# Pacing every load of an attention-plus-FFN kernel by the landing of earlier loads

## The chip, the core and the metric

The kernel runs on one core of a Trainium2 chip. A core has a matrix engine (TensorE, PE in the profile), a vector engine (VectorE, DVE), an activation engine (ScalarE, ACT), GpSimd (POOL) and a queue engine (SyncE, SP); PE, DVE and ACT work on on-chip memory, which 16 DMA engines fill from and empty to device memory (HBM). DMA transfers are issued by an engine's instruction stream: here POOL issues nearly all loads, SP the transposes and stores, ACT a few transfers at the start and one at the end. The metric is the device time of one execution in microseconds (us). Before: 283.06 us, the median of three runs (282.26 to 284.77).

## The reference

Attention with a block mask over 4 batches, 8 heads, 768 positions and 64 channels per head, followed by a gated feed-forward layer on the 3072 rows of 512 channels:

```python
scores = (q @ k.T) / 8                                  # per batch and head, 768 x 768
mask   = |bi - bj| <= 1 or bi, bj in {0, 23} or bj in sampled_blocks[bi]   # blocks of 32
attn   = softmax(where(mask, scores, -1e9)) @ v
x      = attn as (4*768, 8*64)
out    = (sigmoid(x @ w_gate) * (x @ w_val)) @ w_out    # 512 -> 1536 -> 512
```

All inputs but the sampled block numbers are float32, and so is the output. The inputs that are loaded are q, k and v (6.3 MB each) and the three weight matrices (3.1 MB each).

## The kernel before

The matrix products run in float16. The work is cut into 12 units (4 batches by 3 stretches of 256 queries). For each unit and each of 4 pairs of heads, three steps compute scores (`qk`), exponentiate them on ACT (line 570) and multiply by the mask on DVE (line 576; in the first unit the mask is added on PE as a bias instead). Then the product with v, which carries a column of ones for the sum, is taken on PE, divided by that sum on DVE (lines 615 and 616) and transposed into `xT`: by PE in the first two units, after that by a DMA transpose on SP (line 667). The feed-forward part follows in groups of one or two units: `f` multiplies `xT` with columns of `wg` and `wv`, takes tanh on ACT (line 762) and gates on DVE (line 765) into `ht`; `y` multiplies `ht` with `wo`, and ACT or DVE (lines 831 and 833) evacuate the result, which SP stores (line 823). Nearly all matrix products go through the helper `tiled`, so the profile puts them down to line 338.

The order of the instructions on every engine is written out by hand in the string `ORDER`: `Plan.run` walks it and emits each task at its place. A token such as `215@30` means that task 215, a load, also waits for task 30, a score product, so that later batches' loads don't all start at once (`hold`). The order on each engine is thus fixed, and an engine that waits at one instruction holds back all that stand behind it.

Three helpers issue the loads, all on POOL's queue, where each changes float32 to float16 on the way:

- `load_heads` (line 220): two heads of q, k or v. The first batch's q comes in two parts, tiles 0 and 1, and tiles 2 to 5.
- `load_w` (line 230): 256 columns of `wg` and the same 256 of `wv`, two transfers.
- `load_wo` (line 235): four of the twelve row blocks of `wo`.

The loads of the first batch and of the weights are issued up front in the order of the string `FIRST`:

```python
FIRST = "k1 q1 v0 k2 q2 v1 k3 q3 v2 v3 r0 w0 r1 w1 r2 w2 r3 w3 w4 w5 o0 o1 o2"
```

k, q, v and r are k, the first part of q, v and the rest of q, with the number of the pair of heads; w and o are `load_w` and `load_wo`. The first pair's k and q (`kp` in the profile, as they pass through that buffer) come by SP and ACT in float32. Loads of the later batches are tasks of `ORDER`; each waits until its buffer is free, that is, until PE or DVE has read what the last batch left in it (`copies[nm, b - 1, p]`). In batches 1 to 3 a load of q or k is then paired up on DVE (`pair_up`, line 509) and transposed by SP (`xbar`, line 520), and a load of v is copied into `vex` (`vcopy`, line 529). In the first batch, PE transposes q and k (lines 451 and 456).

POOL does nothing in this kernel but set four constants and issue 66 transfers: a small spread matrix (`e<-bb_spread`) and 65 loads. The completion of POOL's transfers is told by eight semaphores, used in turn, so in the program as it is built nearly every transfer from the ninth on waits for the one eight places earlier, besides what its buffer makes it wait for.

Of the kernel before, what the change touches and what calls it, by code (L numbers as in the profile page):

```python
# [22 lines left out]
NT = S // 128  # L23
# [11 lines left out]
BIG = 1024.0  # L35
FIRST = "k1 q1 v0 k2 q2 v1 k3 q3 v2 v3 r0 w0 r1 w1 r2 w2 r3 w3 w4 w5 o0 o1 o2"
FFN_LAG = 3
VW = 96
ORDER = """
j3 j3 j3 j3 0 j3 j3 j3 11D 1:0 8A 3:1 5D 12:2 6:3 4A 7D 2 13A 80:3 106:1 9:0 30:2 107A 10D 81D  # L40
# [114 lines left out]
def kernel(  # L155
# [11 lines left out]
    nc = tc.nc  # L167
# [45 lines left out]
    v16 = sing.tile([128, H, NT, D], f16)  # L213
    vex = [sing.tile([128, H, NT, VW], f16, name=f"vex{r}") for r in range(2)]
    qT = [sing.tile([128, NP, S], f16, name=f"qT{r}") for r in range(2)]
    kT = [sing.tile([128, NP, S], f16, name=f"kT{r}") for r in range(2)]


    def load_heads(dst, src, b, h0, h1, t0=0, t1=NT):
        return nc.gpsimd.dma_start(  # L220
            dst[:, h0:h1, t0:t1, :],
            src[b, h0:h1].rearrange("h (p t) d -> p h t d", t=NT)[:, :, t0:t1, :],
        )

    W_AT = (0, 2, 4, 6, 8, 10, 12)

    def load_w(j):
        f0, f1 = W_AT[j] * 128, W_AT[j + 1] * 128
        for dst, src in ((wg, moe_w_gate), (wv, moe_w_val)):
            nc.gpsimd.dma_start(  # L230
                dst[:, :, f0:f1], src.rearrange("(c p) f -> p c f", p=128)[:, :, f0:f1]
            )

    def load_wo(j):
        nc.gpsimd.dma_start(
            wo[:, 4 * j : 4 * j + 4, :],
            moe_w_out.rearrange("(f p) m -> p f m", p=128)[:, 4 * j : 4 * j + 4, :],
        )

    mc = const[0:NB, 128:].bitcast(f32).rearrange("a (n c) -> a n c", c=4)  # L240
    sbi = sing.tile([NB, 3], mybir.dt.int64)
# [16 lines left out]
    for name in FIRST.split():  # L258
        j = int(name[1])
        if name[0] == "w":  # L260
            load_w(j)
        elif name[0] == "o":
            load_wo(j)
        else:
            dst, src, t0, t1 = {
                "k": (k16, k, 0, NT),
                "v": (v16, v, 0, NT),
                "q": (q16, q, 0, 2),
                "r": (q16, q, 2, NT),
            }[name[0]]  # L270
            load_heads(dst, src, 0, 2 * j, 2 * j + 2, t0, t1)
# [41 lines left out]
    def idle(unit):  # L313
        for i in range(2):
# [4 lines left out]
                start=True,  # L319
                stop=True,  # L320
            )

    def wait_for(ins, earlier, reason):
        tc.add_manual_dep(
            ins,
            earlier.name,
            mybir.DependencyInfo(mybir.DependencyClass.Sync, mybir.DependencyReason.DATA),
            reason=reason,
        )

    plan = Plan(
        ORDER,
        idle,
        lambda load, scored: wait_for(load.ins, scored, "loads spread over the batch before"),
    )

# [3 lines left out]
    def turns(mms, bank, first, begins=True, ends=True):  # L340

        if not first and begins:
            wait_for(nc.tensor.nop().ins, bank.last, "row tiles change banks")
        for n, job in enumerate(mms):
            for row in range(2):
                out, lhsT, rhs = job(row if first else 1 - row, slice(row * D, (row + 1) * D))
                bank.last = tiled(
                    out,  # L350
                    lhsT,
                    rhs,
                    first and begins and n == 0,
                    not first and ends and n == len(mms) - 1,
                )
# [590 lines left out]
    loads = deque()  # L946

    def later(b):
# [3 lines left out]
        def load(nm, p):  # L952
            src, dst = {"k": (k, k16), "q": (q, q16), "v": (v, v16)}[nm]
            ld = plan.add(
                [(DMA, 0.72)],
                lambda eng: load_heads(dst, src, b, 2 * p, 2 * p + 2),
                copies[nm, b - 1, p],
                dma=("L", 0.393),
                gated=True,
            )  # L960
            preps.append(lambda: follow(nm, p, ld))
# [74 lines left out]
    for n in range(1, len(units)):  # L1036
# [5 lines left out]
        for sl in range(6):  # L1042
# [3 lines left out]
            if loads:  # L1046
                loads.popleft()()
            part = parts.popleft() if n > 1 or sl >= FFN_LAG else []
            for i, fn in enumerate(part):
# [53 lines left out]
```

## Time and profile before

| | |
|---|---|
| median of three runs | 283.06 us (282.26 to 284.77) |
| the profiled execution's own time | 281.96 us |
| its span, first to last instruction | 280.2 us |
| PE busy | 272.4 us (97%) |
| DVE / ACT / POOL busy | 187.9 / 192.1 / 47.4 us |
| POOL's queue: packets, data, share of the 16 DMA engines' span | 21552, 13.93 MB, 35.6% |
| SP's and ACT's queue (`hardware_dynamic`, q1) | 34592, 13.99 MB, 22.7% |
| median time from issue to landing: k / q / v | 5.9 / 7.1 / 5.5 us |
| the same for wg / wv / wo | 8.6 / 8.9 / 12.8 us |

The profile is of one execution. "Span" is measured from its first to its last instruction. A row of digits shows the span in 40 slices of 7 us: each digit is the busy share of the slice in tenths. "PEclk" is the share of the full TensorE clock that was granted. The chain that ended last is followed back from the last instruction, at each step to whatever released it. In a list of waits, a row such as `A <- B: 1.1, 1, 1.1` says that A's engine sat idle before A until B released it: 1.1 us in total, once, 1.1 us at the longest. "To landing" is the time from the issue of a transfer to its completion semaphore. In the answer on one tile, `x1: 706/706/706, 31.4 to 31.4` is the number of instructions, their shortest, median and longest duration in ns, and when the first and the last of them started. Matmuls are pipelined and their ends are modelled.

### The profile page before, as it was taken

What the parts mean: (1) busy time and instruction counts of PE and PEld (TensorE: products, weight loads), DVE (VectorE), ACT (ScalarE), POOL (GpSimd) and SP (SyncE); (2) the same over time, 40 slices, a digit from 0 to 9 for tenths busy, and PEclk for the clock granted to TensorE, in tenths of its full rate; (3) what the DMA queues carried; (4) which work ended last, traced back from release to release, by engine and by line L of the source; (5) the groups of instructions that cost most, each with busy time, mean ns of one, the idle gap of its engine ahead of it and who ended that gap; (6) DMA issues with size and microseconds to landing.
All of it is one profiled execution on the core that took longest, in us unless ns stands there. A gap on an engine that the chain in (4) does not pass through costs nothing.

```text
span 280.2 us, 10875 instructions
## 1 busy us (share of the span) xinstructions
PE 272.4 (97%) x4889; PEld 186.1 (66%) x4889; DVE 187.9 (67%) x387; ACT 192.1 (69%) x239; POOL 47.4 (17%) x70
## 2 busy tenths in 40 slices
PE   5999999999999999999999999999999999999995
PEld 2677786777899799766555655666656667555543
DVE  4667894788887888688778746875664888142421
ACT  3798888699897878898668866578677683023301
POOL 8975441011531000082400000000000000000000
PEclk9799999999999999999999999999999999999999
DMA  7999999765589975279967330041100012440003
GB/s 148 184 195 196 200 205 202 110 127 87 77 110 150 206 129 126 40 106 188 125 115 162 68 97 2 12 133 50 30 2 0 6 21 65 117 180 2 0 5 147
DMA packets 56679, 28.92 MB, mean 103 GB/s; under 512 B 33044, under 2 KB 53676, under 8 KB 56632
## 3 DMA queue, kind: packets, MB, share of 16 engines
q0 software_dynamic: 21552, 13.93, 35.6%
q1 hardware_dynamic: 34592, 13.99, 22.7%
q8 instruction: 38, 0.62, 0.9%
q10 hardware_dynamic: 488, 0.30, 0.4%
q14 instruction: 9, 0.07, 0.1%
HBM read 28.47 MB, written 6.29 MB: 124 GB/s over the span
## 4 chain that ended last, share of the span: by engine, by line
PE 91%; DMA 3%; ACT 2%; DVE 2%; issue 1%; SPq 0%; DVEq 0%
PE m L338 89%; DMA xT<-x 2%; DMA e<-bb_spread 1%; ACT P L570 1%; PE m L456 1%; DVE ysb L833 1%; ACT ysb L831 0%; PE m L451 0%; DVE kT L282 0%; DVE mask L282 0%; ACT mask L280 0%; SPq L667 0%; PE m L397 0%; DVE x L616 0%; PE m L315 0%
## 5 line engine op out<-in xcount | busy, mean ns | idle before, releaser
L570 ACT ACTIVATE P<-m 128x1024 f16<-128x1024 f32 x144 | 142.5, 1025 | 31.3 <-PE m L338 27.3
L338 PE MATMUL m<-xT,wv 64*128 64x512 f16 (+2 forms) x672 | 136.1, 331 | 0.3 <-issue 0.3
L338 PE MATMUL m<-xT,wg 64*128 64x512 f16 (+2 forms) x672 | 135.9, 331 | 0.1
L576 DVE TENSOR_TENSOR P<-P,mask 128x1024 f16<-128x1024 f16 x132 | 86.7, 686 | 11.1 <-ACT P L570 10.8
L338 PEld LDWEIGHTS <-wg 64*128 64x128 f16 (+1 forms) x672 | 61.8, 94 | 20.5 <-issue 2.0
L338 PEld LDWEIGHTS <-wv 64*128 64x128 f16 (+1 forms) x672 | 61.8, 94 | 15.9 <-issue 0.3
L338 PE MATMUL m<-wo,ht 64*128 64x512 f16 (+2 forms) x564 | 70.7, 372 | 0.0
L765 DVE SCALAR_TENSOR_TENSOR ht<-th,m 128x512 f16<-128x512 f32 x72 | 49.0, 686 | 30.6 <-ACT th L762 29.6
L762 ACT ACTIVATE th<-m 128x512 f32<-128x512 f32 x72 | 42.7, 598 | 36.0 <-PE m L338 35.3
L338 PE MATMUL m<-qT,kT 64*128 64x256 f16 x576 | 54.0, 272 | 0.3 <-DVE ysb L833 0.2
L338 PEld LDWEIGHTS <-P 64*128 64x128 f16 (+1 forms) x2112 | 46.2, 94 | 9.0 <-issue 1.1
L338 PE MATMUL m<-vex,P 64*128 64x65 f16 (+1 forms) x2112 | 48.2, 190 | 0.0
L338 PEld LDWEIGHTS <-ht 64*128 64x128 f16 (+1 forms) x564 | 30.5, 94 | 21.6 <-issue 1.3
L338 PEld LDWEIGHTS <-kT 64*128 64x128 f16 x576 | 27.4, 95 | 13.0 <-issue 1.7
L220 POOL DMA_DIRECT2D v<-in_v_dram x16 | 11.4, 717 | 65.3 <-PE m L338 56.5
L616 DVE TENSOR_TENSOR x<-m,rz 128x256 f16<-128x256 f32 x48 | 20.4, 425 | 1.7
L615 DVE RECIPROCAL rz<-m 128x4 f32<-128x4 f32 x48 | 8.7, 180 | 17.9 <-PE m L338 16.4
L220 POOL DMA_DIRECT2D q<-in_q_dram x19 | 13.6, 723 | 12.1 <-PE m L338 11.1
L831 ACT ACTIVATE ysb<-m 128x512 f32<-128x512 f32 x13 | 7.5, 597 | 10.6 <-PE m L338 9.9
L833 DVE TENSOR_SCALAR ysb<-m 128x512 f32<-128x512 f32 x9 | 6.1, 688 | 11.8 <-ACT ysb L831 5.5
L220 POOL DMA_DIRECT2D k<-in_k_dram x15 | 10.8, 723 | 6.1 <-PE m L338 5.5
L338 PE MATMUL m<-bias,e 64*128 64x256 f16 x48 | 6.9, 301 | 0.3
(46 smaller groups left out, 69.7 us busy)
## 6 DMA issues: line engine op xcount, KB each, us to landing
out_dram<-ysb SPq DMA_DIRECT2D x23, 256.0 KB, 2.4
v<-in_v_dram POOLq DMA_DIRECT2D x16, 192.0 KB, 5.5
k<-in_k_dram POOLq DMA_DIRECT2D x15, 192.0 KB, 5.9
q<-in_q_dram POOLq DMA_DIRECT2D x12, 192.0 KB, 7.1
wg<-in_moe_w_gate_dram POOLq DMA_DIRECT2D x6, 256.0 KB, 8.6
wv<-in_moe_w_val_dram POOLq DMA_DIRECT2D x6, 256.0 KB, 8.9
wo<-in_moe_w_out_dram POOLq DMA_DIRECT2D x3, 512.0 KB, 12.8
xT<-x SPq DMA_TRANSPOSE x40, 3.2
```

The lines of the kernel that those rows point to most:

```text
L220: return nc.gpsimd.dma_start(dst[:, h0:h1, t0:t1, :], src[b, h0:h1].rearrange("h (p t) d -> p h t d", t=NT)[:, :, t0:t1, :],)
L338: return nc.tensor.matmul(out, lhsT, rhs, start=start, stop=stop, skip_group_check=True).ins
L456: nc.tensor.transpose(out16[a * D : (a + 1) * D, h, i * D : (i + 1) * D], tile_[rows, a], ident[rows, rows],)
L570: nc.scalar.activation(self.pt.rearrange("a h i n -> a (h i n)"), both(self.bank).rearrange("a h n -> a (h n)"), AF.Exp, bias=0.0, scale=SCALE
L576: nc.vector.tensor_tensor(self.pt, self.pt, m.unsqueeze(1).broadcast_to([128, 2, 2, UQ]), op=ALU.mult,)
L615: nc.vector.reciprocal(rz, self.acc[:, :, :, D : D + 1])
L616: nc.vector.tensor_tensor(self.x16.rearrange("a s h d -> a h s d"), self.acc[:, :, :, 0:D], rz.broadcast_to([128, 2, 2, D]), op=ALU.mult,)
L762: nc.scalar.activation(th, both(bank)[:, 0, :], AF.Tanh, bias=0.0, scale=0.5)
L765: nc.vector.scalar_tensor_tensor(self.ht[:, tiles[0] : tiles[-1] + 1, :], in0=th.rearrange("a (f n) -> a f n", n=self.w), scalar=1.0, in1= ...
L831: nc.scalar.activation(ysb, both(bank)[:, s, :], AF.Copy, bias=0.0, scale=0.5)
L833: nc.vector.tensor_scalar(ysb, in0=both(bank)[:, s, :], scalar1=0.5, scalar2=None, op0=ALU.mult)
```

## The change

Every load that goes through the three helpers is now handed to `paced`. It keeps a list, `sent`, of all loads in the order of issue, each with a nominal time in us: 1.0 for two heads (a third of it or two thirds for the parts of the first batch's q), 256/188 = 1.36 for 256 columns of a weight, 2.56 for a part of `wo`. For a new load, `paced` walks back over `sent` and adds up these times; the first load at which the sum of the later ones is at least `AHEAD` = 3.6 is the one whose landing the new load waits for. So at most about five loads of heads, four to five of weights, or three of `wo` are in flight.

The wait stands on POOL's queue, in front of the load, beside the waits for its buffer and for its semaphore. `FIRST`, `ORDER`, the buffers, the sizes of the transfers and everything on the other engines stay as they are. In the program as it is built, k3 (the seventh load) is the first that waits for another, for k1; the number of POOL's instructions is the same, and so are the order and the waits on PE, DVE, ACT and SP.

```diff
+AHEAD = 3.6
...
+    sent = []
+
+    def paced(load, us):
+
+        left = 0.0
+        for earlier, t in reversed(sent):
+            if left >= AHEAD:
+                wait_for(load.ins, earlier, "loads in flight")
+                break
+            left += t
+        sent.append((load.ins, us))
+        return load
+
     def load_heads(dst, src, b, h0, h1, t0=0, t1=NT):
-        return nc.gpsimd.dma_start(
+        load = nc.gpsimd.dma_start(
             dst[:, h0:h1, t0:t1, :],
             src[b, h0:h1].rearrange("h (p t) d -> p h t d", t=NT)[:, :, t0:t1, :],
         )
+        return paced(load, 1.0 * (t1 - t0) / NT)
...
     def load_w(j):
         f0, f1 = W_AT[j] * 128, W_AT[j + 1] * 128
         for dst, src in ((wg, moe_w_gate), (wv, moe_w_val)):
-            nc.gpsimd.dma_start(
+            load = nc.gpsimd.dma_start(
                 dst[:, :, f0:f1], src.rearrange("(c p) f -> p c f", p=128)[:, :, f0:f1]
             )
+            paced(load, (f1 - f0) / 188)
...
     def load_wo(j):
-        nc.gpsimd.dma_start(
+        load = nc.gpsimd.dma_start(
             wo[:, 4 * j : 4 * j + 4, :],
             moe_w_out.rearrange("(f p) m -> p f m", p=128)[:, 4 * j : 4 * j + 4, :],
         )
+        paced(load, 2.56)
```

`wait_for`, which adds such a wait, stood further down and is moved up unchanged.

More of the change, by code (lines that the diff above doesn't have):

```diff
@@ L216, with wait_for @@
     kT = [sing.tile([128, NP, S], f16, name=f"kT{r}") for r in range(2)]
+    def wait_for(ins, earlier, reason):
+        tc.add_manual_dep(
+            ins,
+            earlier.name,
+            mybir.DependencyInfo(mybir.DependencyClass.Sync, mybir.DependencyReason.DATA),
+            reason=reason,
+        )
+    sent = []
[8 more added lines that the diff above has]
+        return load
     def load_heads(dst, src, b, h0, h1, t0=0, t1=NT):
-        return nc.gpsimd.dma_start(
+        load = nc.gpsimd.dma_start(
             dst[:, h0:h1, t0:t1, :],
@@ L321, in idle @@
             )
[L323 to L329, printed above, removed]
     plan = Plan(
```

## The prediction

> **What bounds the kernel now.** I read the page's busy row first, then the chain that ended last, then the waits of POOL (the only queue that the change touches), and last, for each load, when POOL issued it and how long it took to land.
>
> ```profile
> span 280.2 us, 10875 instructions
> PE 272.4 (97%) x4889; PEld 186.1 (66%) x4889; DVE 187.9 (67%) x387; ACT 192.1 (69%) x239; POOL 47.4 (17%) x70
> ...
> PEclk9799999999999999999999999999999999999999
> DMA  7999999765589975279967330041100012440003
> ...
> PE 91%; DMA 3%; ACT 2%; DVE 2%; issue 1%; SPq 0%; DVEq 0%
> ```
>
> TensorE is busy for 97% of the span and holds 91% of the chain; the loads are on the chain only with the small `e<-bb_spread` transfer of the first 5.6 us, which the change leaves alone. Among PE's own waits the only DMA is that one, 0.8 us. So a load matters only if it lands after the instruction that reads it was due. The DMA row is at 9 from slice 2 to slice 7: for the weights, the limit is transfer rate, not issue.
>
> The transfers of the stretch from 8 to 45 us, asked for by themselves:
>
> ```profile
> DMA packets 12126, 7.32 MB, mean 198 GB/s; under 512 B 998, under 2 KB 12120, under 8 KB 12120
> ...
> q0 software_dynamic: 12120, 7.23, 136.6%
> ```
>
> Nothing but POOL's queue moves data there (the other rows of that answer are instruction fetches of 0.09 MB), at a steady 198 GB/s; SP issues nothing between 1.65 and 46.5 us.
>
> How deep is the queue now? POOL's waits say that a limit is already there:
>
> ```profile
> POOL wo L235 <- DMA wg<-in_moe_w_gate_dram: 1.1, 1, 1.1
> ...
> POOL q L220 <- DMA wo<-in_moe_w_out_dram: 0.8, 1, 0.8
> POOL wg L230 <- DMA v<-in_v_dram: 0.7, 1, 0.7
> ```
>
> These are loads that waited for the one eight places earlier: eight completion semaphores, used in turn. So before has up to eight loads in flight, not an unlimited number. What that depth does is seen in the time to landing of one load on a full and on an empty queue (the k load issued at 31.4 us, the v load issued at 120.1 us):
>
> ```profile
> L220 POOL DMA_DIRECT2D k<-in_k_dram x1: 706/706/706, 31.4 to 31.4; - x1
> DMA to landing us min/median/max: 13.0/13.0/13.0
> ```
>
> ```profile
> L220 POOL DMA_DIRECT2D v<-in_v_dram x1: 707/707/707, 120.1 to 120.1; - x1
> DMA to landing us min/median/max: 3.5/3.5/3.5
> ```
>
> The same bytes, 13.0 and 3.5 us: the difference is time spent behind other loads.
>
> **The change, step by step.** *The rule.* Each load walks back over the loads before it, adds their nominal times until 3.6 us is reached, and waits for the next one back. Loads of two heads (1.0 each) wait for the fifth before them, with 4.0 us of queued work still ahead; weight columns (1.36 each, mixed with q parts of 0.67) have 4.1 to 4.75 ahead; wo (2.56 each) 3.9 to 5.1; the first batch's loads 3.67 to 4.3.
>
> *Are the nominal times right?* Issue plus time to landing gives landings at 42.4, 43.4, 44.4, 45.4, 46.3, 47.3 and 48.3 us for seven loads of heads (1.0 apart), 23.7 and 25.1 for a wg and its wv (1.34), 36.3, 38.9 and 41.5 for wo (2.6). Yes.
>
> *Does the queue run dry?* Four loads on an empty queue took 3.5 (120.1 us), 3.6 (71.9), 3.7 (61.1) and 3.8 (81.7); less 1.0 of transfer, a load needs a lead of about 2.6 us. With 3.67 or more ahead it comes 1.0 us before the engines need it. No weight load stands alone in this trace; its lead lies between the 2.6 of the heads and the 5.3 that the first wg leaves (6.7 to landing at 10.4 us, less 1.36, but that one stood behind others). I take 2.6, since the lead is what is left after the bytes. Going through the 65 loads in order (issue at the awaited landing plus 0.06, at least 0.70 after the issue before it; landing at the old landing, or at issue + 2.6 + nominal time, whichever is later):
>
> - k3: issue 6.45 becomes 7.75; 7.75 + 3.6 = 11.35, old landing 12.42, spare 1.07.
> - v2: 7.97 becomes 9.28; spare 0.84.
> - last wg: 22.77 becomes 27.75; 27.75 + 3.96 = 31.7 against 32.46, spare 0.74, the least of the weights.
> - last wo: 27.98 becomes 33.8; 39.0 against 41.48, spare 2.5.
> - batch 1, first k: 28.96 becomes 36.4; 40.0 against 42.40, spare 2.4.
> - the burst at 120 to 128 us: the sixth to eleventh load are issued up to 3 us later; least spare 1.4.
>
> Some 38 of the 65 issues move, by up to 7.5 us, and no landing does. The rest (61 to 119 us, and from 133) are released by PE, DVE or a buffer, at times when the fifth load before has long landed. Behind a waiting load on POOL stand only later loads. The order of instructions is the same on all five engines, and the waits of PE, DVE, ACT and SP are unchanged. POOL's number of instructions is unchanged too; its idle time just moves in between.
>
> *What covers it if I am a little wrong?* Landing and first reader, in us: k3 12.4 and 13.95; third q part (r2) 22.4 and 24.8; wg/wv columns 3 28.4 and 31.6; columns 5 33.8 and 38.7; wo 0 36.3 and 41.5; wo 2 41.5 and 45.5; first q of batch 1 43.4 and its pairing copy 46.1. The least is 1.5 (k3), so all loads could land 1 us later at no cost.
>
> *What might be gained?* The SP transposes and stores share the DMA engines. But in their stretches (from 46.5 us) the loads in flight are the same: by 46.5 the queue holds four heads loads under either rule, and the five issued at 81.7 to 84.6 keep their issue times. POOL's issues and DVE collide seldom: one value copy took 576 ns beside a median of 352, so 0.2 us, off the chain. I cost it at nothing, bounds -0.3 and, by the cover above, +0.5.
>
> *Sum:* 281.96 (span 280.2 and 1.8 around it) + 0 = 282.0 on the profiled execution. It lies 1.1 below the median of 283.06, and the three runs spread over 2.5 us, so on the median: **283.0**, own range 282.0 to 284.6.
>
> **The rivals.**
> *Refill too slow (slower).* If a load that is issued on demand needs much more than 2.6 us of lead, the queue runs dry once per group and the slip adds up. The same walk with a lead of 4.4 brings the last wo to 44.1, still before 45.5; with 4.9 to 47.0 (1.5 us late); with 5.4 to 50.05, 4.5 late, r2 to 26.5 (1.7 late). So it costs over 1% from a lead of about 5.1, twice the measured one; at 5.4, **about 287.5**. For it: the first six loads took 5.1 to 5.7 to land with little of POOL's own ahead. Against: they shared the engines with five transfers of SP and ACT, and four loads alone needed 3.5 to 3.8. One way to it is that DVE holds up POOL while it writes descriptors; against that, POOL's issues last 698 to 870 ns although DVE is busy for 27.7 of the 37 us from 8 to 45. The Trainium skill (SBUF — State Buffer, "SBUF: two separate sides") warns of just this: while VectorE runs a two-port operation GpSimd can't write descriptors, and the DMA waits; its example, 620 ns turned into 3100, would make an estimated 0.7 us issue 3.5 and the lead 5.4, and by that rule the time would be this rival's. The trace's 870 ns at most doesn't agree.
> *The other queues are relieved (faster).* If a shallower POOL queue let SP's transfers through sooner, the most on the chain is the 5.5 us of `xT<-x` from 88.2 us; transposes on quiet engines land in 2.3. At best 5.5 - 2.3 = 3.2 us: **279.8**. Against: PE's idle just there is 0.1 us, and the loads in flight then don't change.
> *The limit does nothing, since eight semaphores limit already.* Then POOL's issue times stay: also 283.0. Against: eight loads are 8 to 10 us of work, the new limit 4 to 5.
>
> **How the numbers follow.** Forecast 0.76, limit without effect 0.04 (both no change), refill too slow 0.12, relief 0.08. Faster by over 1%: 0.08; within 1% (2.8 us, about what a measurement here tells from nothing): 0.80; slower: 0.12. The range takes in the bounds of the unknown costs and half of the run spread on both sides, and reaches a little towards both rivals: 281.2 to 285.3.
>
> **What the changed profile would show.** Right: the median time to landing of the wg, wv and wo loads falls from 8.6, 8.9 and 12.8 to some 5.5, 5.5 and 6.5; the last wo is issued near 33.8 and lands near 41.5; 8 to 45 us still moves about 198 GB/s; POOL's waits for DMAs rise from 6 to some 15 us in sum; PE's busy time and the chain stay. Wrong: GB/s below 185 in that stretch, wo 2 landing after 45.5, PE waits on `wo`, `wg` or `k`; or, on the other side, `xT<-x` landing clearly sooner. Also a different granted clock (now 0.57 from 8 to 11 us) could move the time by 1 us with no load involved.

## The result, and the profile after

The changed kernel takes **285.44 us** (median of 20 runs, 283.36 to 289.99) against 283.10 for the kernel before (20 runs, 281.73 to 286.39). The ratio is **1.0071, 95% interval 1.0047 to 1.0095**: some 2 us slower, where 283.0 and a range up to 285.3 were predicted. The ratio is taken from the fast runs (three runs, over 1.5% above the fastest of their kernel, are left out), and isn't the quotient of the two medians. The profiled execution took 285.12 us, with a span of 283.4.

The busy row, the DMA row and the chain by engine, from the page of the kernel after:

```profile
span 283.4 us, 10877 instructions
PE 271.5 (96%) x4889; PEld 187.2 (66%) x4889; DVE 186.8 (66%) x387; ACT 192.4 (68%) x239; POOL 47.3 (17%) x70
...
DMA  7999999996399694359985530052100011340003
...
PE 87%; DMA 6%; ACT 2%; issue 2%; DVE 2%; POOL 1%; DVEq 0%
```

The added code moves the line numbers on by 17, so L355 is L338 of before. PE has the same 4889 products and 0.9 us less busy time; the 3.2 us are idle time of PE. The chain gave 4 points of PE's share to DMA (3% to 6%) and "issue". In the DMA row, the block of nines reaches to slice 9, two further than before: the same bytes took longer. The transfers from 8 to 45 us, asked for by themselves as in the prediction:

```profile
DMA packets 11053, 6.55 MB, mean 177 GB/s; under 512 B 935, under 2 KB 11046, under 8 KB 11046
...
q0 software_dynamic: 11046, 6.45, 128.4%
```

177 GB/s for 198. POOL's queue also holds less of the 16 engines' time (128.4% for 136.6%; over 100% because packets of one engine overlap). So the engines were without work more often, at a time when loads were always outstanding. In time to landing, the groups of DMA issues of the page:

```profile
wg<-in_moe_w_gate_dram POOLq DMA_DIRECT2D x6, 256.0 KB, 5.9
wv<-in_moe_w_val_dram POOLq DMA_DIRECT2D x6, 256.0 KB, 6.0
wo<-in_moe_w_out_dram POOLq DMA_DIRECT2D x3, 512.0 KB, 8.3
```

Each load lands sooner after its issue than before (8.6, 8.9 and 12.8), but it is issued later by more than that. Issue and landing of some loads, before and after, in us:

| load | issue before, after | landing before, after | slip |
|---|---|---|---|
| k3 | 6.45, 7.71 | 12.42, 12.35 | -0.1 |
| first wg | 10.36, 11.46 | 17.06, 17.82 | 0.8 |
| last wv | 24.01, 30.56 | 33.77, 36.46 | 2.7 |
| wo 0 | 25.35, 32.14 | 36.31, 40.42 | 4.1 |
| wo 1 | 26.08, 35.39 | 38.91, 43.46 | 4.6 |
| wo 2 | 27.98, 36.74 | 41.48, 45.99 | 4.5 |
| first k of batch 1 | 28.96, 40.95 | 42.40, 47.05 | 4.7 |
| last k of batch 1 | 42.93, 50.46 | 50.55, 55.98 | 5.4 |

The slip starts with the pacing and grows along the list in steps: 0.3 to 0.7 us at single loads, 1.4 at wo 0. What it costs is in PE's waits (us in total, times, longest):

```profile
PE m L355 <- DMA wo<-in_moe_w_out_dram: 1.8, 1, 1.8
PE m L355 <- issue: 1.7, 2, 1.3
...
PE m L355 <- DVE ht L782: 0.7, 2, 0.5
```

and, for the first and the third row, in PE's timeline (start, duration, what; the idle time before it and its releaser in brackets):

```profile
40.47 1.04 PE L355 MATMUL m<-wo,ht 64*128 64x512 f16 x8
41.34 0.38 PE L355 MATMUL m<-qT,kT 64*128 64x256 f16 x4
43.50 0.82 PE L355 MATMUL m<-wo,ht 64*128 64x512 f16 x6 [1.78 <-DMA wo<-in_moe_w_out_dram]
```

```profile
57.02 0.39 PE L355 MATMUL m<-qT,kT 64*128 64x256 f16 x4 [0.46 <-DVE ht L782]
57.62 0.40 PE L355 MATMUL m<-qT,kT 64*128 64x256 f16 x4 [0.20 <-DVE ht L782]
```

The first `y` reaches the rows of wo 1 with nothing else to do, and they land at 43.46. The scores at 57 us wait for the last k of batch 1, though the row names DVE's `ht`. The chain, in order of time (start, duration, what), shows how:

```profile
40.95 6.09 DMA k<-in_k_dram
...
50.46 5.52 DMA k<-in_k_dram
...
56.01 0.04 DVE kp L526
56.05 0.24 issue
56.28 1.29 DVE ht L782 x2
```

The k load that was issued at 50.46 lands at 55.98, and pairing it up on DVE holds the two gates (`ht`) behind it on that queue, which hold PE.

The row "issue" of 1.7 us is two pauses of PE (1.33 at 86.71 and 0.37 at 92.36) for which no semaphore is recorded; before had one of 0.28. Together: 1.78 + 0.66 + (1.70 - 0.28) = 3.9 us of new waiting, less 1.1 us by which the first weight product starts earlier (23.89 for 25.02; in the profile of before the granted clock was 0.57 from 8 to 11 us, here 1.00). That leaves 2.8 of the 3.2 us by which the spans differ. The earlier start of this execution is mostly lost again at wo 1, which comes when it comes.

The change was run again and profiled at the same clock as before (its expectation stands in the next section). Its PE waits and its transfers from 8 to 45 us:

```profile
PE m L355 <- DMA wo<-in_moe_w_out_dram: 1.0, 1, 1.0
...
PE m L355 <- DVE ht L782: 0.6, 2, 0.4
PE m L355 <- issue: 0.5, 1, 0.5
```

```profile
DMA packets 10952, 6.46 MB, mean 175 GB/s; under 512 B 932, under 2 KB 10946, under 8 KB 10946
```

There the first weight product starts at 25.02, as before, the wo parts land at 41.12, 43.69 and 46.22, and 1.0 + 0.6 + (0.5 - 0.3) = 1.8 us of PE's waits stand against a span that is 2.0 longer (282.2 against 280.2). So most of the loss is **loads that land up to 5 us late**, 1.0 of it at `wo` and 0.6 at batch 1's k. The question left is why they are late, with four to five loads always in the queue.

### The profile page after: what moved, and what is told of

Its sections match the earlier page's. It is cut to its first block, busy times and chain, and to the rows that moved or that the text cites. A ratio compares the mean times of both kernels' runs of the same rounds, so it can differ in the third digit from the quotient of the medians.

```text
span 283.4 us, 10877 instructions
## 1 busy us (share of the span) xinstructions
PE 271.5 (96%) x4889; PEld 187.2 (66%) x4889; DVE 186.8 (66%) x387; ACT 192.4 (68%) x239; POOL 47.3 (17%) x70
## 4 chain that ended last, share of the span: by engine, by line
PE 87%; DMA 6%; ACT 2%; issue 2%; DVE 2%; POOL 1%; DVEq 0%
PE m L355 86%; DMA k<-in_k_dram 4%; DMA e<-bb_spread 1%; ACT P L587 1%; PE m L473 1%; DVE ysb L850 0%; POOL q L242 0%; DVE ht L782 0%; ACT ysb L848 0%; ACT mb L305 0%; ACT mask L305 0%; PE m L414 0%; DVE kT L307 0%; POOL v L242 0%; DVE x L633 0%
## 5 line engine op out<-in xcount | busy, mean ns | idle before, releaser
L355 PE MATMUL m<-xT,wv 64*128 64x512 f16 (+2 forms) x672 | 136.2, 331 | 1.7 <-issue 1.7
L355 PE MATMUL m<-xT,wg 64*128 64x512 f16 (+2 forms) x672 | 135.9, 331 | 0.0
L355 PEld LDWEIGHTS <-wg 64*128 64x128 f16 (+1 forms) x672 | 61.8, 94 | 21.6 <-issue 3.6
L355 PE MATMUL m<-wo,ht 64*128 64x512 f16 (+2 forms) x564 | 70.8, 372 | 1.8 <-DMA wo<-in_moe_w_out_dram 1.8
L355 PEld LDWEIGHTS <-wv 64*128 64x128 f16 (+1 forms) x672 | 61.9, 94 | 15.2
L779 ACT ACTIVATE th<-m 128x512 f32<-128x512 f32 x72 | 42.7, 598 | 37.2 <-PE m L355 36.4
L355 PE MATMUL m<-qT,kT 64*128 64x256 f16 x576 | 53.5, 269 | 1.0 <-DVE ht L782 0.7
L355 PEld LDWEIGHTS <-P 64*128 64x128 f16 (+1 forms) x2112 | 46.4, 94 | 8.9 <-issue 1.3
L355 PE MATMUL m<-vex,P 64*128 64x65 f16 (+1 forms) x2112 | 48.3, 190 | 0.0
L355 PEld LDWEIGHTS <-ht 64*128 64x128 f16 (+1 forms) x564 | 30.9, 94 | 23.3 <-issue 3.2
L355 PEld LDWEIGHTS <-kT 64*128 64x128 f16 x576 | 27.5, 94 | 13.5 <-issue 2.6
L355 PE MATMUL m<-bias,e 64*128 64x256 f16 x48 | 6.0, 272 | 0.5
```

The lines of the kernel that those rows point to most:

```text
L355: return nc.tensor.matmul(out, lhsT, rhs, start=start, stop=stop, skip_group_check=True).ins
L779: nc.scalar.activation(th, both(bank)[:, 0, :], AF.Tanh, bias=0.0, scale=0.5)
```

## The experiments

Three theories were put on record first. **L**: a load's lead (issue to landing, less its transfer) grows with its size, so that weights need more than the 2.6 us that heads showed. **U**: the lead is 2.6, but the 16 engines don't finish together; instruction fetches hold one engine for about 1 us, and a shallow queue passes that on. **D**: DVE keeps POOL from writing descriptors. After the first runs two more: **R**, an engine that has run through its share restarts slowly, so that the engines drift apart and a shallow queue gives each delay to all of them; and **M**, that the count of nominal times fails only where loads of different sizes follow one another.

**Loads alone, in six passes.** The 29 loads of the first batch and the weights and batch 1's eight k and q loads, 37 in all, nominally 41.4 us; the attention and feed-forward work is left out:

```diff
+    one_pass(None)           # no pacing
+    one_pass(3.6)            # as the change
+    one_pass(0.0)            # one load at a time
+    one_pass(None, pe=800)   # beside a stream of products on PE
+    one_pass(3.6, pe=800)
+    one_pass(3.6, dve=120)   # beside f16 copies on DVE
```

> The loads alone, without the computation (the output is zeros): six passes over the 29 loads of the first batch and the weights and eight loads of heads, one pass after another. Pass 1: no pacing (the eight semaphores alone). Pass 2: paced at 3.6. Pass 3: one load at a time. Pass 4: no pacing, beside a stream of 800 matmuls of 128 columns. Pass 5: paced at 3.6 beside the same stream. Pass 6: paced at 3.6 beside 120 copies of 128x768 float16 on DVE. By their nominal times the 37 loads are 41.4 us. Theory L (a load's lead grows with its size): alone, heads land in 3.6, a weight's columns in about 5.9 and a part of wo in about 8.3 us; pass 2 is 3 to 5 us longer than pass 1, most of it at wo; passes 4 and 5 differ in the same way. Theory U (a load needs 2.6 us of lead whatever its size, but the 16 engines do not finish their shares together, and a fetch of instructions holds one engine for 0.95 us): alone, a weight's columns land in 4.0 and wo in 5.2 us; pass 2 is within 1 us of pass 1, since nothing fetches instructions; pass 5 is 2 to 4 us longer than pass 4. Theory D (DVE keeps POOL from writing descriptors): pass 2 as pass 1, pass 5 as pass 4, pass 6 over 3 us longer than pass 2.

Busy time in each pass, from its first issue to its last landing (stretch, length, then PE, PEld, DVE, ACT and POOL busy, clock, mean share of the DMA engines, which passes 1 where packets overlap, GB/s):

```profile
1.24:48.08 46.84, 0.00 (x0) 0.00 (x0) 0.79 (x2) 0.78 (x1) 27.00 (x37) 1.00 1.26 179
48.37:100.34 51.97, 0.00 (x0) 0.00 (x0) 0.00 (x0) 0.00 (x0) 26.89 (x37) 1.00 1.18 162
100.63:246.79 146.16, 0.00 (x0) 0.00 (x0) 0.00 (x0) 0.00 (x0) 26.81 (x37) 1.00 0.45 57
247.08:295.41 48.33, 46.12 (x800) 45.94 (x798) 0.00 (x0) 0.00 (x0) 26.87 (x37) 1.00 1.24 176
295.93:348.31 52.38, 44.37 (x795) 44.19 (x792) 0.00 (x0) 0.00 (x0) 26.88 (x37) 0.97 1.19 162
348.85:399.96 51.11, 0.00 (x0) 0.00 (x0) 46.98 (x119) 0.00 (x0) 27.68 (x37) 0.50 1.20 164
```

The loss is there with nothing but loads on the chip: 51.97 for 46.84 us, 5.1 us or 11%. The third pass gives the time to landing of a load that is quite alone:

```profile
L244 POOL DMA_DIRECT2D k<-in_k_dram x7: 696/713/716, 100.6 to 239.8; - x7
DMA to landing us min/median/max: 3.4/3.4/3.6
```

```profile
L253 POOL DMA_DIRECT2D wg<-in_moe_w_gate_dram x6: 740/757/760, 139.9 to 191.3; - x6
DMA to landing us min/median/max: 3.7/3.9/4.0
```

```profile
L259 POOL DMA_DIRECT2D wo<-in_moe_w_out_dram x3: 740/740/740, 199.4 to 211.3; - x3
DMA to landing us min/median/max: 5.6/5.6/5.7
```

Less the nominal times of 1.0, 1.36 and 2.56 that is a lead of 2.4, 2.5 and 3.0. **L falls**: the 2.6 of the prediction was right to within 0.4 for all three. D falls too, since pass 2 loses without DVE: with DVE busy for 46.98 of 51.11 us the paced pass takes 51.1, without it 52.0, and POOL's 37 issues 27.7 and 26.9 us. Of U the fetches fall, since pass 2, in which no other engine runs a program and only one fetch of 8 KB falls, loses 5.1 us against its unpaced partner, and pass 5, beside PE's stream, 4.1. Left of U is that the engines don't finish together.

Where pass 2 loses: not evenly. Most loads land at their nominal distance; single ones come 0.6 to 1.6 us later than it (v3, the first wg, two more w, wo 0). And two things take part. The share of the DMA engines falls from 1.26 to 1.18, 6%: idle engines. GB/s divided by that share falls from 142 to 137, 3%: slower packets. The trace has the packets one by one: of the 13312 of POOL's queue in a pass, with a median of 60 ns, 43 took over 200 ns in the unpaced pass (31 of them in its first 5 us), 143 at 3.6, and 325 with one load at a time, four in five of these 1 to 2 us after an issue, when the engines start on an empty queue.

One more thing takes part. Once in most passes of this program and of the next one with loads alone, POOL issues a load 0.5 to 1.4 us later than any of its waits explains. In pass 2 it is v3 (at 57.59, 1.0 us late), and the jumps at v3 and at the first wg behind it make 2.2 of the 5.1 us; on an unpaced queue such a pause costs nothing that shows. In the first 38 loads of the changed kernel there is no such pause: an issue that waited for a landing comes 0.28 or 0.53 us after it. So the kernel loses without it.

**Three kernels with the whole work**: the limit at 6.0 in place of 3.6; `wo` without pacing; and only the loads of batches 1 to 3 paced.

```diff
-AHEAD = 3.6
+AHEAD = 6.0
```

> AHEAD 6.0 in place of 3.6, nothing else: seven loads of heads, five to six of weights, three to four of wo in flight. L: the longest lead (5.7 for wo) is covered, so every load lands as before the change, the last wo at 41.5 to 42 us, and the time is that of before: ratio 1.000 (0.998 to 1.002). U: most, but not all of the slip goes; last wo at 42.5 to 44; since wo may be 4 us late at no cost, the time is 283.1 to 284, ratio 1.000 to 1.003.

```diff
-    def paced(load, us):
+    def paced(load, us, held=True):
...
-            if left >= AHEAD:
+            if left >= AHEAD and held:
...
-        paced(load, 2.56)
+        paced(load, 2.56, held=False)
```

> Paced at 3.6 as in the change, except the three wo loads, which wait for no other load. L and U alike: the weights' columns are as late as in the change (last wv near 36.5), but the wo loads follow them at 2.6 us each and land near 39.1, 41.7 and 44.3, so PE's wait of 1.8 us for wo goes, and the first loads of batch 1 land 2.7 and not 4.6 us late: ratio 1.001 to 1.004, time 283.4 to 284.2. If the loss has nothing to do with these landings, 1.007 as in the change.

```diff
+        held = len(sent) >= len(FIRST.split()) + 6     # the 29 first loads go free
...
-            if left >= AHEAD:
+            if left >= AHEAD and held:
```

> Only the loads of batches 1 to 3 are paced at 3.6; the first batch and the weights go as before the change. L and U: wo lands at 41.5, nothing waits, ratio 1.000 (0.998 to 1.003), time 283.1. If the later batches' pacing is what costs, 1.004 to 1.007.

The transfers from 8 to 45 us of these three, in this order:

```profile
DMA packets 12034, 7.26 MB, mean 196 GB/s; under 512 B 992, under 2 KB 12028, under 8 KB 12028
```

```profile
DMA packets 11285, 6.72 MB, mean 181 GB/s; under 512 B 948, under 2 KB 11279, under 8 KB 11279
```

```profile
DMA packets 11939, 7.19 MB, mean 194 GB/s; under 512 B 990, under 2 KB 11933, under 8 KB 11933
```

| | ratio to before (95%) | wo lands | PE's new waits |
|---|---|---|---|
| limit 6.0 | 1.0021 (0.9995 to 1.0046) | 36.8, 39.3, 41.9 | none for a load |
| wo free | 1.0032 (1.0005 to 1.0058) | 39.7, 42.2, 44.7 | 0.1 at the scores of batch 1, 0.6 for `xT` at 94 us |
| late loads only | 1.0018 (0.9985 to 1.0052) | 37.2, 39.7, 42.2 | none |

At 6.0 the rate is back and so is the time. With the later batches alone paced nothing waits, and the time is that of before within the noise. That speaks for a loss that comes with the pacing of the first batch and the weights, though the interval would allow 0.5% for the later loads. With `wo` free the heads and columns still lose their 2 to 3 us (last wv at 36.97 for 33.77), the wo parts land in time for `y`, and the 1.0 us at `wo` is gone. That PE's wait at `wo` follows from late landings is thereby shown; that all of the loss does is not, since the intervals of these runs overlap.

**How deep must the queue be, and with which loads?** Loads alone again: the mixed list at six limits, then heads, columns and parts of wo by themselves, unpaced and at 3.6. The rest of the work is left out.

```diff
+    for ahead in (None, 2.6, 3.6, 4.6, 5.6, 7.0):
+        mixed(ahead)
+    for kind in (heads, columns, rows_out):
+        for ahead in (None, 3.6):
+            kind(ahead)
```

> Loads alone again, nothing else running (the output is zeros). Six passes over the same 37 loads, with no pacing and with AHEAD 2.6, 3.6, 4.6, 5.6 and 7.0; then 48 loads of heads, 24 of weight columns and 12 of wo, each without pacing and with 3.6. Theory R (an engine whose own ring ran empty starts again with slow packets, and the 16 engines do not finish a load together; a shallow queue hands every such delay of one engine to all 16, since the next load waits for the last of them): the pass gets longer the shallower the queue is: over the unpaced one about +10 us at 2.6, +5 at 3.6, +2 to 3 at 4.6, under 1.5 at 5.6 and under 0.5 at 7.0; and the loads of one kind alone lose too, 5 to 12% of their pass. Theory M (the count by nominal times only fails where the size changes, as from v to r to w and from w to wo): the heads, the columns and wo alone lose under 2%, and the mixed passes lose about 5 us at 3.6 and 4.6 alike.

The passes in that order (stretch, length, DVE, ACT and POOL busy, clock, share of the DMA engines, GB/s; the passes at 5.6 and 7.0 and the two of wo are left out):

```profile
1.26:48.38 47.12, 0.14 (x1) 0.77 (x1) 26.95 (x37) 1.00 1.26 178
48.67:107.23 58.56, 0.00 (x0) 0.00 (x0) 26.84 (x37) 1.00 1.11 143
107.52:157.88 50.36, 0.00 (x0) 0.00 (x0) 26.87 (x37) 1.00 1.22 167
158.17:205.25 47.08, 0.00 (x0) 0.00 (x0) 26.89 (x37) 1.00 1.26 178
...
301.46:352.44 50.98, 0.00 (x0) 0.00 (x0) 34.31 (x48) 1.00 1.23 185
352.73:409.40 56.67, 0.00 (x0) 0.00 (x0) 34.30 (x48) 1.00 1.18 167
409.69:445.43 35.74, 0.00 (x0) 0.00 (x0) 17.80 (x24) 1.00 1.33 176
445.71:485.30 39.59, 0.00 (x0) 0.00 (x0) 17.79 (x24) 1.00 1.23 159
```

Mixed: 47.1 without pacing, 58.6 at a limit of 2.6, 50.4 at 3.6, **47.1 at 4.6**, 47.7 at 5.6 and at 7.0. At 3.6 the mixed list takes 7% longer (11% in the program before this one), heads alone 11%, columns alone 11%, parts of wo 1% (34.33 for 33.97). M falls, for a list of one kind loses as much. What decides is the work that is really ahead: at 3.6 the heads and columns stop at the first sum that reaches it, 4.0 and 4.1 us, and lose; wo stops at 5.1 and loses 1%. At 4.6 it is 5.0 for heads and 4.67 at the least in the mixed list, and nothing is lost. So by these single passes the bound lies between 4.1 and about 4.7 us of work, some 2 us above the lead of one load. R gave the direction, but 2 to 3 us of loss at 4.6 that aren't there.

The heads' pass shows the form. Unpaced, they land every 0.97 to 1.0 us. Paced, most distances are 0.95 to 1.1 too, with single jumps of 1.6 to 2.3 among them. During the largest (379 to 381.6 us) the engines together still move 173 GB/s, for 185 in the unpaced pass. A load is complete with the last of 16 increments of its semaphore, and of that load 15 had come by 380.67 and the last at 381.60. It is not a queue that runs empty as a whole, then, and not a longer lead of each load: one share of a load comes late while the others are done. Slow packets: 45 in the unpaced mixed pass, 280 at 2.6, 130 at 3.6, 56 at 4.6; heads 46 and 209.

**The change again, and two more limits.**

> The changed kernel once more, to see which of its stalls come again. If they are the pacing's: PE waits 1 to 2.5 us for wo near 43 us and 0.3 to 1 us for the first scores of batch 1 near 57 us, 8 to 45 us moves 172 to 184 GB/s, ratio 1.005 to 1.010. The pause of 1.3 us near 86.7 us, which no semaphore ended, has no tie to pacing if it is 0.2 to 0.5 us this time, as in the four other profiles.

285.05 against 282.79, ratio 1.0094 (1.0054 to 1.0133); its rows stand in the section above.

```diff
-AHEAD = 3.6
+AHEAD = 4.6
```

> AHEAD 4.6 in the whole kernel: six loads of heads in flight, five of weight columns, three to four of wo, at least 5.0 us of queued work ahead of a load of heads and 4.75 to 6.1 ahead of the weights. If the threshold that the loads alone showed (a loss at 4.0 us ahead, none at 5.0) is what decides: 8 to 45 us at 192 to 198 GB/s, under 25 packets of over 200 ns in that stretch, last wo at 41.5 to 42.7, no wait of PE for wo, ratio 1.000 (0.998 to 1.003). If the waits on POOL cost something of themselves, or if two and a half times the lead is not enough beside the computation: last wo at 43.5 to 45, ratio 1.003 to 1.006.

```diff
-AHEAD = 3.6
+AHEAD = 2.6
```

> AHEAD 2.6 in the whole kernel, the lead of a load that is alone: four loads of heads, three of columns, two to three of wo in flight. If the walk of my prediction were right, a queue with 3.0 us ahead and a lead of 2.6 would still never run dry and the time would be 283. By the loads alone (last wo 7 us later than at 3.6): last wo at 50 to 53 us, the columns 4 and 5 at 37 to 42 (due at 36.3 and 38.7), PE waits of 7 to 10 us in sum at wg, wv, wo and the first scores of batch 1, ratio 1.02 to 1.035.

Transfers from 8 to 45 us at 4.6 and at 2.6, and PE's waits at 2.6:

```profile
DMA packets 12070, 7.28 MB, mean 197 GB/s; under 512 B 996, under 2 KB 12064, under 8 KB 12064
```

```profile
DMA packets 9888, 5.45 MB, mean 147 GB/s; under 512 B 897, under 2 KB 9882, under 8 KB 9882
```

```profile
PE m L355 <- DMA wo<-in_moe_w_out_dram: 3.8, 2, 2.5
PE m L355 <- issue: 1.9, 1, 1.9
...
PE m L473 <- DMA q<-in_q_dram: 1.6, 1, 1.6
PE m L355 <- DVE ht L782: 0.9, 2, 0.7
...
PE m L355 <- DMA wv<-in_moe_w_val_dram: 0.6, 1, 0.6
```

| limit | GB/s, 8 to 45 us | slow packets there | last wo lands | ratio to before (95%) |
|---|---|---|---|---|
| none (before) | 198 | 7 of 11634 | 41.5 | 1 |
| 6.0 | 196 | 9 of 11546 | 41.9 | 1.0021 (0.9995 to 1.0046) |
| 4.6 | 197 | 12 of 11580 | 41.8 | 1.0005 (0.9973 to 1.0036) |
| 3.6 (the change) | 177, 175 | 76 of 10623, 69 of 10530 | 46.0, 46.2 | 1.0071 (1.0047 to 1.0095) |
| 2.6 | 147 | 156 of 9497 | 51.7 | 1.0306 (1.0268 to 1.0344) |

At 4.6 all the waits on POOL's queue are there and the time is that of before: the waits themselves cost nothing that shows, the depth does. At 2.6 the loss is 0.0306 x 283 = 8.7 us, of which 3.8 + 1.6 + 0.9 + 0.6 = 6.9 (7 to 10 were expected) are PE's waits for loads or for what a late load holds up.

## Why the prediction was wrong

- **"Does the queue run dry?"** is the step that failed. Its lead of 2.6 us measured 2.4 to 3.0. What did not follow from it is "with 3.67 or more ahead it comes 1.0 us before the engines need it". A load lands with the last of 16 increments, and the step treated 16 engines as one queue that is empty only when all are. The runs showed that lists of loads with 4.0 to 4.1 us of work ahead take 11% longer (the mixed list, with 3.7 us or more, 7 and 11%), and with 4.67 or more no longer. So "no landing moves" became a slip of 4.6 us at wo 1 and 5.4 at batch 1's last load. The four loads of 3.5 to 3.8 us from which the lead came could not show it, as each stood on an empty queue. A fifth could: the v load issued at 64.92, alone on POOL's queue but beside SP's transposes, took 5.7 us in the trace of before. Of its 16 increments 15 had come by 69.12, and the last at 70.58.
- **"What covers it"** held as a list. Slips of 0.8 to 2.7 at the r and w loads stayed under their covers of 2.4 to 4.9 and cost nothing. wo 1, due at 42.60 with 3.7 of cover, slipped by 4.8 in the profile at before's clock (43.69) and cost 1.0. wo 0 slipped just to its due time (41.12 and 41.52). The list ended at batch 1's first q; the last k, with a slip of 5.4, cost 0.66 more.
- **"Are the nominal times right?"** held on a full queue: at 6.0 the wo parts land 2.5 apart, for 2.6 before.
- **The walk of the issues** was right in kind: the loads wait on POOL with nothing behind them but loads, PE's order and busy time are unchanged. Its 0.06 us from the awaited landing to the issue was too small: it is 0.28 and at some loads 0.53, as it was already in the trace of before at loads that waited for the one eight places earlier. Its times came late with the landings that they await: the last wo issued at 36.7 (33.8 predicted), POOL's waits for DMAs 23 us in sum (15), landing medians 5.9, 6.0 and 8.3 (5.5, 5.5 and 6.5).
- **Refill too slow** (0.12) was the way it went, at a smaller price: in its walk, wo 2 at 46.0 falls between a lead of 4.4 (44.1) and 4.9 (47.0), about 4.7, whereas 287.5 was worked out for 5.4. But the lead that it assumed isn't there, and the one way to it that was named falls. With 120 copies on DVE (395 ns for 768 f16 a partition) beside the loads the paced pass was not longer, and an issue took 27.7/37 = 0.75 us for 0.73. The Trainium skill (SBUF — State Buffer, "SBUF: two separate sides") has VectorE's two-port operations keep GpSimd from writing descriptors. No run here shows that; which mode these copies ran in, the trace doesn't tell.
- **Other queues relieved** (0.08) didn't show: `xT<-x` took 2.9 us to landing for 3.2, but the list of PE's waits names it neither before nor after, and `qT<-qp` and `kT<-kp` took longer (3.9 and 4.5 us for 2.8 and 3.2). **The limit does nothing** (0.04) is wrong for 3.6: the wg loads alone went from 8.6 us to landing to 5.9.
- The signs named as "wrong" were the right ones to look for: 177 GB/s is below 185, the last wo lands at 45.99, after 45.5, and PE waits on `wo`.

**What the cause is, and what isn't known.** Shown: with too little work ahead (4.0 to 4.1 us) loads take longer, with or without the other engines' work; the DMA engines' busy share falls while loads are outstanding, and more packets are slow. In the kernel the rate falls with the limit, 197, 177 and 147 GB/s at 4.6, 3.6 and 2.6, and PE's waits for late loads rise with it. Argued only: that an engine that is done with its share waits until the slowest has finished, because the next load is released by the landing, and starts slowly again. What fits it: the Trainium skill (DMA: Bandwidth & Descriptors, "Why a DMA increments its semaphore by 16 and not by 1") says that the 16 engines of such a load finish independently and that only the sixteenth increment means that all data is there. The trace agrees in this: it has 16 completion packets per load, and where one load lands late, up to 15 of the next load's 16 are already done (on the unpaced queue too).

What the trace has besides is how far apart a load's first and last increments are. From the first wv to the second k of batch 1 the median is 1.2 us before and 2.0 in the changed kernel; in the passes with loads alone it is 1.4 for heads at 3.6, 0.7 for wo at 3.6 and 1.3 for the mixed list at 4.6. An estimate from these: at the issue, 0.3 us after the awaited landing, the engine that is furthest ahead has about 4.0 - 0.3 - 1.4 = 2.3 us of heads left, less than their lead of 2.4, so it runs dry. For wo it has 5.1 - 0.3 - 0.7 = 4.1, and in the mixed list at 4.6 at least 4.67 - 0.3 - 1.3 = 3.1, more than any lead here, and 1% or nothing is lost there. The engine that is last has 3.4 us left even at the least depth of 3.67: if the 16 engines were one queue, it would never run dry. This fits the step between 4.1 and 4.7, but is an estimate. The records don't name the engine, so which one is last, and whether it is always the same, stays open, and so does why a restart is slow. Not settled either is PE's pause without a semaphore, 1.7 us in the profile of after. It was 0.3 before, 0.5 in the change run again, 1.5 at 4.6, where the time is that of before, and 1.9 at 2.6, so it doesn't go with the pacing in these runs. It is left out of the loss.

## What to carry to other kernels

The depth at which a DMA queue keeps its rate can't be read from the time of one load alone: here a load needed about 2.5 us of lead, and the queue between 4.1 and 4.7 us of work ahead. That a load lands with the last of its 16 increments, up to 2.6 us after the first, fits this, as far as an estimate goes. Where a limit on transfers in flight is wanted, measure the list of loads by itself at a few depths, look at the rate, and count what the granularity really leaves ahead (4.0 and 5.1 us under the same 3.6). Then set the slip of each load against the time at which its first reader is due; a slip of 2.7 us cost nothing in this kernel and one of 4.8 cost 1.0.

## What was not expected of the hardware

- The step is steep: with 4.0 to 4.1 us of queued work a list of loads takes 11% longer, with 4.67 to 5.0 no longer, and the mixed list at a limit of 2.6 (three loads of heads ahead) takes 24% longer (58.56 for 47.12 us).
- The first packets on an empty queue are slow: 325 of 13312 packets over 200 ns with one load at a time, 43 unpaced, at a median of 60 ns.
- The time of a load that is alone grows less than its size: 3.4 us for 192 KB, 3.9 for 256 KB, 5.6 for 512 KB.
- The 16 shares of a load don't finish together even on a full queue: before, between 18 and 45 us, the first and the last increment were 1.2 to 1.3 us apart at all loads but one (1.8).
